# Hash-bucketed attention with two mixing layers: reciprocals spread a period later, bits placed a period earlier, x loaded through GpSimd's queue, three transpose banks

## The chip, the cores and the metric

The kernel runs on one core of a Trainium2 chip. The metric is the device time of one execution in microseconds (us), the median of several runs. The engines are TensorE (PE in the profile, PEld for its weight loads), VectorE (DVE), ScalarE (ACT), GpSimd (POOL) and SyncE (SP), which here only issues DMAs. GpSimd issues DMAs too, from the same in-order instruction stream in which it computes.

## What is computed

Everything is float32. Attention has batch 2, 8 heads, 768 positions and head size 64; a key counts for a query only if both fall in the same of 64 hash buckets:

```python
q_bits = (einsum('bhsd,dk->bhsk', q, proj) > 0)      # 6 bits
k_bits = (einsum('bhsd,dk->bhsk', k, proj) > 0)
mask = q_bucket[:, :, :, None] == k_bucket[:, :, None, :]
scores = where(mask, scale * q @ k.T, -1e9)
attn = exp(scores - max); attn = attn / (sum(attn) + 1e-9)
x = attn @ v                                          # -> (2, 768, 512)
xk, xr = mix of x with x shifted by one position
x = sigmoid(xr @ w_r) * (relu(xk @ w_k) ** 2 @ w_v)
h = relu(x @ w_in); u, v = halves of h
out = (u * (w_spatial @ layernorm(v) + b_spatial)) @ w_out
```

## The kernel before

Two stages follow each other: `attention` and `mixers`. Attention treats the 16 heads as 8 pairs. A pair has 12 units: two halves of the 768 queries, two heads e, and three blocks of 128 queries each, so 96 units in all; six units (one pair, one half) form a group g. Work goes in 32 periods of three units: the loop `for p in range(np3)` (L516) writes out by hand the order of every engine's instructions, each engine works its own stream in order, and a pair takes periods 4n to 4n+3.

For one unit, `scores` (L314) multiplies in TensorE into a bank pair of `ps_s`; the operands in `TK` hold the head's values in two parts, and the bits of the buckets in spare rows, so that one product gives score and mask. `peak` and `bias` (L330, L339) take the maximum on VectorE while copying the scores out of PSUM; `expo` (L345) is the exponential on ScalarE with the row sums in `den`; `transp` (L357) transposes three blocks of 128x128 into one bank of `ps_t`, and `evac` (L365) copies that bank out on ScalarE. A unit has two such moves. `ps_t` has two banks. `av` (L391) multiplies with v into one of two output banks, `obank[g % 2]`, twelve matmuls a period (`av3`), and lags by three periods. `recip` (L375) takes the reciprocals of a group's row sums on VectorE, transposes them, writes them to DRAM in four small DMAs (tile `ds`) and reads them back in two, spread over partitions (tile `rb`); `finish` (L401) multiplies them into the output bank on VectorE.

For a pair to come, `load_x` (L236, one DMA on SP, one buffer) and `load_pair` (L241, four DMAs on GpSimd) fetch it; `split_piece` (L254, eight on GpSimd) makes the low parts. `bits_mm` (L271) projects x in TensorE into `obank[0]`, `bits_sign` (L279, VectorE) makes bits of it (tile `zb`), `bits_scale` (L285, GpSimd) scales them (`zc`), and `bits_place` (L290) copies them into `TK` with eight DMAs on SP. SP's stream holds, in this order of planning: ds and rb, weight loads, placed bits, x and v; a DMA whose wait isn't over holds up those behind it.

Between these steps stands other work, put into half periods by `at_slot(p, k, job)` (L416): 12 weight blocks of the mixers (`weight_jobs`, L30: load, ScalarE and VectorE steps, the last two on GpSimd), two more in the last periods, and the first block of the mixers' inputs (`mix_jobs`, L130: `before`, a multiplication, on GpSimd; `full` on VectorE; `parts` on ScalarE and GpSimd). `bank` (L162) gives the mixers their output banks in turn from `ps_s`, `ps_t` and `obank`.

## Time and profile before

| | us |
|---|---|
| runs shown | 593.57, 601.83, 590.88 |
| median | 593.57 |
| profiled execution, its own time | 593.77 |
| its span on the core | 592.0 |

The span is what the trace covers, from its first to its last instruction; times of rows are counted from its start. A row of the timeline has start, length, engine, line, operation, output and inputs, a count of merged instructions, and in brackets the idle time before it with what ended it. A wait is put down to what came last.

### The profile page before, as it was taken

The numbers are of one execution on the slowest core, as the hardware profiler recorded it, in microseconds if no ns is written. First come the engines' busy times: TensorE is split into PE (matmuls) and PEld (weight loads), VectorE is DVE, ScalarE is ACT, GpSimd is POOL, SyncE is SP. The second block draws the span as 40 slices with busy tenths as digits, with TensorE's granted clock in tenths as the row PEclk, the third lists the DMA queues.
The fourth block names the chain that finished last, engine by engine and source line by source line (L and its number), as shares of the span: only waits on it lengthen the run. The fifth ranks groups of instructions, "written<-read, shape, count | busy, mean of one in ns | idle before, by whom it ended". The sixth has DMA issues, their size and how long they took to land.

```text
span 592.0 us, 8973 instructions
## 1 busy us (share of the span) xinstructions
PE 555.9 (94%) x3188; PEld 471.3 (80%) x3188; DVE 375.7 (63%) x804; ACT 337.8 (57%) x718; POOL 147.9 (25%) x154
## 2 busy tenths in 40 slices
PE   6879997998999899889979999999999999999997
PEld 5766665666666566658979999999999899999996
DVE  6547985776757687953986557342799687272240
ACT  1867887677777778854965275643743552221112
POOL 5554576265636473540000000000020000000000
PEclk8889999899999999989989999999999999999999
DMA  8984295619293923102222021100175210001102
GB/s 166 223 169 127 63 234 97 171 48 219 74 195 98 197 62 99 40 1 85 73 71 72 2 71 37 37 1 1 37 227 179 66 53 2 0 2 54 53 19 89
DMA packets 21245, 51.96 MB, mean 88 GB/s; under 512 B 3840, under 2 KB 6864, under 8 KB 21200
## 3 DMA queue, kind: packets, MB, share of 16 engines
q1 hardware_dynamic: 15584, 36.42, 20.7%
q0 software_dynamic: 5472, 14.94, 13.1%
q8 instruction: 25, 0.41, 0.3%
q14 instruction: 20, 0.16, 0.1%
q10 hardware_dynamic: 144, 0.02, 0.0%
HBM read 47.08 MB, written 3.19 MB: 85 GB/s over the span
## 4 chain that ended last, share of the span: by engine, by line
PE 67%; DVE 9%; DMA 9%; ACT 7%; issue 4%; POOL 3%; SPq 1%; POOLq 0%; DVEq 0%; ACTq 0%
PE o L176 16%; PE v L626 8%; PE s L324 7%; PE t L362 6%; PE s L176 6%; PE o L393 5%; PE k L176 5%; DMA tk<-zc 5%; PE w L176 4%; PE u L176 4%; PE r L176 3%; DVE p L334 3%; PE o L626 3%; DMA w_raw<-in_w_k_dram 2%; ACT PT L368 2%
## 5 line engine op out<-in xcount | busy, mean ns | idle before, releaser
L334 DVE TENSOR_SCALAR_CACHE_REDUCE p<-s 128x768 f32<-128x768 f32 x96 | 91.5, 953 | 58.4 <-PE s L324 53.9
L368 ACT COPY PT<-t 128x384 f32<-128x384 f32 x192 | 84.8, 475 | 45.4 <-PE t L362 45.3
L362 PE MATMUL t<-ident,p 128*128 128x128 f32 x576 | 85.2, 285 | 17.2 <-ACT PT L368 16.4
L324 PE MATMUL s<-tk 128*128 128x384 f32 x384 | 89.6, 367 | 10.3 <-DMA tk<-zc 7.3
L352 ACT ACTIVATE p<-p,nb 128x768 f32<-128x768 f32 x96 | 90.2, 940 | 12.9 <-DVE nb L342 12.1
L324 PEld LDWEIGHTS s<-tk 128*128 128x128 f32 x384 | 66.9, 197 | 34.9 <-issue 9.7
L362 PEld LDWEIGHTS t<-ident,p 128*128 128x128 f32 x576 | 67.0, 144 | 32.0 <-ACT PT L368 25.8
L393 PE MATMUL o<-PT,v 128*64 128x384 f32 x384 | 69.6, 499 | 0.0
L258 POOL TENSOR_TENSOR tk<-x,tk 64x384 fp32r<-64x384 f32 x56 | 58.5, 1070 | 31.7 <-DMA x<-in_kq_dram 23.6
L626 PE MATMUL v<-k,wv 128*128 128x384 f32 x288 | 53.9, 335 | 0.6 <-DVE k L592 0.6
L626 PEld LDWEIGHTS v<-k,wv 128*128 128x128 f32 x288 | 50.3, 188 | 0.9 <-DVE k L592 0.9
L393 PEld LDWEIGHTS o<-PT,v 128*64 128x64 f32 x384 | 25.0, 138 | 29.2 <-issue 29.1
L685 POOL DMA_DIRECT2D wsp<-in_w_spT_dram x6 | 3.6, 606 | 174.8 <-DVE w_a L44 168.3
L176 PE MATMUL k<-tk,wk 128*128 128x384 f32 x252 | 45.5, 334 | 0.0
L176 PE MATMUL o<-wk,tk 128*128 128x512 f32 (+1 forms) x204 | 44.8, 377 | 0.0
L176 PEld LDWEIGHTS k<-tk,wk 128*128 128x128 f32 x252 | 43.9, 188 | 0.0
L176 PEld LDWEIGHTS o<-wk,tk 128*128 128x128 f32 x204 | 36.8, 188 | 6.9
L592 DVE TENSOR_TENSOR k<-kt,k 128x384 fp32r<-128x384 f32 x32 | 17.8, 556 | 22.1 <-ACT k L610 22.0
L176 PE MATMUL r<-tk,wr 128*128 128x384 f32 x144 | 27.7, 342 | 3.0 <-DVE tk L122 1.9
L150 DVE SCALAR_TENSOR_TENSOR f<-XT,msc,d 128x384 f32<-128x384 f32 x32 | 21.2, 661 | 13.7 <-ACT d L144 9.0
L121 ACT CAST tk<-g 128x384 fp32r<-128x384 f32 x16 | 8.2, 515 | 37.5 <-DVE g L756 37.5
L176 PEld LDWEIGHTS r<-tk,wr 128*128 128x128 f32 x144 | 25.1, 189 | 5.3 <-DVE tk L122 2.4
(107 smaller groups left out, 892.4 us busy)
## 6 DMA issues: line engine op xcount, KB each, us to landing
tk<-in_kq_dram POOLq DMA_DIRECT2D x32, 384.0 KB, 7.3
x<-in_kq_dram SPq DMA_DIRECT2D x8, 768.0 KB
w_raw<-in_w_k_dram SPq DMA_DIRECT2D x8, 512.0 KB
w_raw<-in_w_v_dram SPq DMA_DIRECT2D x8, 512.0 KB
w_raw<-in_w_in_dram SPq DMA_DIRECT2D x8, 512.0 KB
v<-in_vP_dram SPq DMA_DIRECT2D x8, 384.0 KB
rb<-ds SPq DMA_DIRECT2D x32, 96.0 KB
out_dram<-ot SPq DMA_DIRECT2D x11, 256.0 KB
```

What stands on the lines that cost most here:

```text
L121: nc.scalar.copy(hi, src)
L150: nc.vector.scalar_tensor_tensor(st["f"], x, mu, st["d"], op0=ALU.mult, op1=ALU.add)
L176: nc.tensor.matmul(o, a, x, start=(i == 0), stop=(i == len(seq) - 1))
L258: nc.gpsimd.tensor_sub(tk[l, 1 + 2 * t, o], raw[pp][l, t, o], tk[l, 2 * t, o])
L324: nc.tensor.matmul(s[:, c, :HS], w, t[:, n, c * HS:(c + 1) * HS], start=(n == 0), stop=(n == 1),)
L334: nc.vector.tensor_scalar(c, s[:, :, :HS], -BIG / 2, None, op0=ALU.max, op1=ALU.max, accum_out=m)
L352: nc.scalar.activation(c, c, AF.Exp, bias=nb, scale=0.125, accum_out=den[g][:, u:u + 1])
L362: nc.tensor.transpose(t[:, 128 * n:128 * n + 128], p[:, k0:k0 + 128], ident)
L368: nc.scalar.copy(PT[g][:, e, 3 * c:3 * c + 3, 128 * j:128 * j + 128], t[:, :HS].rearrange("p (n q) -> p n q", n=3),)
L393: nc.tensor.matmul(obank[g % 2][64 * e:64 * e + 64, :HS], vt[g // 2][:, kt, e, :], PT[g][:, e, kt, :], start=(kt == 0), stop=(kt == 5),)
L592: later(lag, lambda: eng.tensor_sub(lo, src, hi))
L626: nc.tensor.matmul(os[m][:, :HS], w, x, start=(c == 0 and k == 0), stop=(c == 7 and k == 2),)
```

## The change

Six things change. `ps_t` gets a third bank and `obank` is one bank instead of two; the bits' product goes to a `ps_t` bank, and the mixers' rotation `bank` is adapted. `load_x` goes through GpSimd's queue for pairs 2 to 7. `recip` ends with the write of ds; the read of rb becomes `spread`, one period later, on SP, and `recip` stands ahead of the jobs of its half period. `finish` moves from the first half of period 2g+5 to the second half of 2g+4. The bits' steps move forward: product, sign and scale to the first half of the pair's second period (they were in the second half of the second and the first half of the third), the placing to the second half of the second period (was the third). The first mix block's `before` goes from GpSimd to VectorE, with lags of 0, 0 and 1 half periods instead of 0, 1 and 2.

```diff
-    ps_t = ctx.enter_context(tc.tile_pool(name="ps_t", bufs=2, space=PS))
+    ps_t = ctx.enter_context(tc.tile_pool(name="ps_t", bufs=3, space=PS))
-    obank = [ps_o.tile([128, 512], F32, name=f"o{n}") for n in range(2)]
+    obank = ps_o.tile([128, 512], F32, name="o0")
...
-        n = turn[0] % (2 if turn[0] < 8 else 3)
+        n = turn[0] % (2 if turn[0] < 8 else 6)
...
-        if n == 0:
+        if n % 3 == 0:
             return ps_s.tile([128, 2, 512], F32, tag="s", name=name)[:, 0, :]
-        if n == 1:
+        if n != 2:
             return ps_t.tile([128, 512], F32, tag="t", name=name)
-        return obank[turn[0] // 3 % 2]
+        return obank
...
-            nc.sync.dma_start(raw[pp], kq[b, p].rearrange("t r s -> r t s"))
+            (nc.gpsimd if pp > 1 else nc.sync).dma_start(raw[pp], kq[b, p].rearrange("t r s -> r t s"))
...
         def bits_mm(pp):
+            zs[pp] = ps_t.tile([128, 512], F32, tag="t", name="z")
             for g in range(4):
...
-                    obank[0][32 * g:32 * g + 32, :HS], pb, raw[pp][:, 1 - g // 2, o:o + HS],
+                    zs[pp][32 * g:32 * g + 32, :HS], pb, raw[pp][:, 1 - g // 2, o:o + HS],
...
                 nc.sync.dma_start(ds[:, 32 * n:32 * n + 32], rt[32 * n:32 * n + 6, :])
+            R[g] = ds
+
+        def spread(g):
+            ds = R[g]
             R[g] = at.tile([128, 3, 128], F32, tag="rb", bufs=2, name="rb")
...
-                    obank[g % 2][64 * e:64 * e + 64, :HS],
+                    obank[64 * e:64 * e + 64, :HS],
...
-            jobs = mix_jobs(mid, 0, which, 4 * which, 2, nc.gpsimd)
-            for job, lag in zip(jobs[3 * c:3 * c + 3], (0, 1, 2)):
+            jobs = mix_jobs(mid, 0, which, 4 * which, 2, nc.vector)
+            for job, lag in zip(jobs[3 * c:3 * c + 3], (0, 0, 1)):
...
-                at_slot(p0 + 1, 1, lambda n=pp + 1: bits_mm(n))
-                at_slot(p0 + 2, 0, lambda n=pp + 1: bits_sign(n))
-                at_slot(p0 + 2, 0, lambda n=pp + 1: bits_scale(n, nc.gpsimd))
-                at_slot(p0 + 2, 1, lambda n=pp + 1: bits_place(n))
+                at_slot(p0 + 1, 0, lambda n=pp + 1: bits_mm(n))
+                at_slot(p0 + 1, 0, lambda n=pp + 1: bits_sign(n))
+                at_slot(p0 + 1, 0, lambda n=pp + 1: bits_scale(n, nc.gpsimd))
+                at_slot(p0 + 1, 1, lambda n=pp + 1: bits_place(n))
...
             if p >= 3:
                 av3(p - 3)
-            if p >= 5 and p % 2:
-                finish((p - 5) // 2)
+            if p >= 2 and p % 2 == 0:
+                recip(p // 2 - 1)
             for job in plan.pop((p, 0), ()):
                 job()
-            if p >= 2 and p % 2 == 0:
-                recip(p // 2 - 1)
+            if p >= 3 and p % 2:
+                spread((p - 3) // 2)
...
             score(a + 2)
             expo(a + 2)
+            if p >= 4 and p % 2 == 0:
+                finish((p - 4) // 2)
...
         r_group(0, 1, mid)
+        spread(np3 // 2 - 1)
         av3(np3 - 2)
```

The warm-up matmuls and the sign follow the renamed banks and are left out here.

## Rows read from the trace of the kernel before

**Rows 1.** The page's first part: busy time, share of the span and instructions of each engine.
```profile
PE 555.9 (94%) x3188; PEld 471.3 (80%) x3188; DVE 375.7 (63%) x804; ACT 337.8 (57%) x718; POOL 147.9 (25%) x154
```
**Rows 2.** Busy time by stretch (start:end, length, then busy us and instructions of each engine, TensorE's granted clock as a share of full speed, mean busy share of the DMA engines, GB/s).
```profile
50.00:250.00 200.00, 183.09 (x1152) 126.91 (x1152) 150.48 (x363) 152.60 (x341) 108.26 (x105) 0.99 0.51 121
...
265.00:592.00 327.00, 319.97 (x1747) 304.49 (x1745) 187.62 (x357) 146.11 (x295) 3.60 (x6) 0.99 0.17 56
```
**Rows 3.** Waits between 40 and 250 us: who waited for whom, us in total, times, the longest.
```profile
PE t L362 <- ACT PT L368: 11.3, 29, 2.4
```
**Rows 4.** The timeline of TensorE's matmuls: the bits' product at the end of period 21, the first rows of periods 22 and 23, the second half of period 23, and the first row of period 24.
```profile
179.25 0.85 PE L274 MATMUL o<-x,msc 128*32 128x384 f32 x8
180.03 1.68 PE L324 MATMUL s<-tk 128*128 128x384 f32 x8
...
186.98 1.64 PE L324 MATMUL s<-tk 128*128 128x384 f32 x8
...
191.29 0.98 PE L324 MATMUL s<-tk 128*128 128x384 f32 x4
192.10 0.82 PE L362 MATMUL t<-ident,p 128*128 128x128 f32 x6
193.16 0.93 PE L362 MATMUL t<-ident,p 128*128 128x128 f32 x6 [0.24 <-ACT PT L368]
193.85 1.64 PE L324 MATMUL s<-tk 128*128 128x384 f32 x8
```
**Rows 5.** The same timeline where periods 4, 12, 21 and 25 begin and where the next ones do (period 22 begins in the second line of rows 4).
```profile
40.27 0.60 PE L324 MATMUL s<-tk 128*128 128x384 f32 x2
...
48.91 1.65 PE L324 MATMUL s<-tk 128*128 128x384 f32 x8
...
100.37 0.60 PE L324 MATMUL s<-tk 128*128 128x384 f32 x2
103.95 2.29 PE L324 MATMUL s<-tk 128*128 128x384 f32 x6 [2.98 <-DMA tk<-zc]
...
111.85 1.64 PE L324 MATMUL s<-tk 128*128 128x384 f32 x8
...
171.10 0.77 PE L324 MATMUL s<-tk 128*128 128x384 f32 x3
...
200.75 0.59 PE L324 MATMUL s<-tk 128*128 128x384 f32 x2
...
211.14 1.66 PE L324 MATMUL s<-tk 128*128 128x384 f32 x8
```
**Rows 6.** Busy time by stretch as in rows 2, of two slices of 5 us.
```profile
65.00:70.00 5.00, 4.76 (x31) 2.97 (x31) 4.90 (x10) 3.59 (x9) 4.84 (x5) 1.00 0.49 159
...
105.00:110.00 5.00, 5.00 (x26) 3.42 (x26) 3.48 (x11) 2.70 (x6) 0.00 (x0) 0.81 1.07 312
```
**Rows 7.** The timeline of SP's queue: DMAs issued, with the time that issuing took.
```profile
166.09 0.46 SPq L239 DMA_DIRECT2D x<-in_kq_dram  x1
...
189.60 6.23 SPq L305 DMA_DIRECT2D tk<-zc  x8
...
198.82 1.30 SPq L383 DMA_DIRECT2D ds<-rt  x4
207.48 1.13 SPq L386 DMA_DIRECT2D rb<-ds  x2
```
**Rows 8.** The timeline around period 17: SP's issue of a weight block for it, and TensorE.
```profile
135.93 0.39 SPq L37 DMA_DIRECT2D w_raw<-in_w_k_dram  x1
...
140.35 1.66 PE L324 MATMUL s<-tk 128*128 128x384 f32 x8
...
148.67 0.93 PE L362 MATMUL t<-ident,p 128*128 128x128 f32 x6 [2.36 <-ACT PT L368]
...
150.31 1.66 PE L324 MATMUL s<-tk 128*128 128x384 f32 x8
```
**Rows 9.** Single lines of the kernel: least, median and greatest length in ns of GpSimd's tk issues (each 384 KB, half of an x load), the time from issue to landing of all 32 tk loads (the line of the view for that tile), and three VectorE operations: one with one input, f of the mix, and finish.
```profile
L246 POOL DMA_DIRECT2D tk<-in_kq_dram x16: 583/632/742, 1.2 to 194.4; - x16
...
DMA to landing us min/median/max: 4.3/7.3/12.8
...
L62 DVE TENSOR_SCALAR w_p<-w_b x32: 412/419/1126, 45.2 to 455.6; 128x512 uint32<-128x512 uint32 x32
...
L150 DVE SCALAR_TENSOR_TENSOR f<-XT,msc,d x32: 600/618/1354, 231.8 to 391.8; 128x384 f32<-128x384 f32 x32
...
L406 DVE TENSOR_TENSOR XT<-o,rb x16: 533/558/561, 52.2 to 270.2; 128x384 f32<-128x384 f32 x16
```
**Rows 10.** The timeline of GpSimd: the first piece that waits for x (period 21), the scaling of bits in period 22, and the first tk issue in period 23.
```profile
175.99 4.77 POOL L258 TENSOR_TENSOR tk<-x,tk 64x384 fp32r<-64x384 f32 x4 [9.87 <-DMA x<-in_kq_dram]
...
185.15 1.24 POOL L287 TENSOR_SCALAR zc<-zb,msc 128x384 fp32r<-128x384 f32 x1 [4.39 <-issue]
...
193.17 0.66 POOL L246 DMA_DIRECT2D tk<-in_kq_dram  x1
```
**Rows 11.** The timeline of VectorE and TensorE in period 31, the last of attention.
```profile
254.61 0.94 DVE L334 TENSOR_SCALAR_CACHE_REDUCE p<-s 128x768 f32<-128x768 f32 x1
...
251.97 0.96 PE L324 MATMUL s<-tk 128*128 128x384 f32 x4
...
257.29 1.54 PE L362 MATMUL t<-ident,p 128*128 128x128 f32 x6 [2.52 <-ACT PT L368]
```
## What the change should do to the time

> **What bounds the kernel now.** I read the page's busy shares first [rows 1], then the busy times by stretch [rows 2], then TensorE's waits inside attention, and last TensorE's rows in order of time. The first says TensorE, the second more: after 265 us it is busy 319.97 of 327 us, and the change alters only which bank the groups rotate through there, so that stage keeps its time. Between 50 and 250 us TensorE is busy 183.09 of 200 us, while ScalarE has 152.60 and VectorE 150.48. So nearly all that can be won is TensorE's idle time in attention (17 us in those 200) and the slow clock after long idle stretches.
>
> The timeline [rows 4] shows one period p of three units (p = 23, from the 8 score products at 186.98 to those at 193.85: 6.87 us, my base). The reader is to see the one break of TensorE's work in it: 6 transposes end, then 0.24 us until ScalarE has emptied a transpose bank. Bits add 0.78 us once in four periods (179.25 to 180.03). Summed from 40 to 250 us that wait is 11.3 us in 29 times [rows 3], once in each period and two more. The other wait, for placed bits, is in the next part [rows 5].
>
> **What is removed: the bits' wait.** Length of the four periods with such a wait, less 6.87 and less 0.78 for bits where they are computed [rows 4, 5]: p4 48.91 - 40.27 = 8.64, over by 1.77; p12 111.85 - 100.37 = 11.48, over by 4.61 (2.98 idle, and then the next 6 score products take 2.29 us where 6 of 8 take about 1.2: the granted clock is 0.81 of 2.4 GHz from 105 to 110 [rows 6], so part ran at 1.2 GHz); p21 180.03 - 171.10 = 8.93, over by 1.28; p25 211.14 - 200.75 = 10.39, over by 2.74. Sum 10.4 us.
> Why they wait: GpSimd scales the bits at 185.15 (1.24 us) [rows 10], SP begins to place them only at 189.60, and needs 6.23 us for 8 placements [rows 7]; the first half is wanted from 193.85 on, the second from 200.75, when p25 begins. p25 runs over by 2.7, so the last, issued at 195.1, is down only about 203.4, 8.3 us later. In the changed order z is computed behind av, at +4.3 us in its period (where scores(a+2) stood, 191.29 - 186.98 [rows 4]), plus 0.8, 0.6 for the sign (as f, of as many columns [rows 9]) and 1.24 for the scale: placing begins about 7 us into period 4n-3 and ends at 13.3; even with 8.3 us to land the first half is down at 18.4 and the second at 21.6, while they are wanted at 20.6 and 27.5. The tk and x loads, beside which it took so long, now come later than the placements, so it should land sooner. Taken: all 10.4 us; bounds 5.9 (p4 and p25 stay) and 10.4.
>
> **The transposes' third bank.** Two banks make the third transpose group wait for the first one's copy. With three it starts at once; the fourth then asks for the first bank 0.41 us later (6 transposes, 0.82 us for two groups [rows 4]), when its copy, late by 0.24, is done. TensorE gains 0.24 per period. Some of the 29 are longer and have other causes (the longest, 2.4, is costed below), so I count 26 plain periods of the 29 from 3 to 31: 26 x 0.24 = 6.2; I take 6.0. Bounds: nothing, if ScalarE or VectorE set the period instead, and 7.5. z now takes a turn in the same banks; its reader, the sign, is through 0.6 us after bits, under scores and one transpose group (0.98 + 0.4): no cost. The one output bank left: finish(g) now stands in the second half of period 2g+4 and av of the next group in the first half of 2g+5, some 4 us of scores and transposes later [rows 4]: no cost while rb is there.
>
> **SP without x and without the wait for ds.** Spread no longer holds SP until ds lands (198.82 to 207.48 is the case [rows 7]), and x leaves SP's queue. In p17 ScalarE's copies, and through them TensorE for 2.36 us, wait behind a step on a weight block that SP issued at 135.93, right behind x [rows 8]: that period is 150.31 - 140.35 - 0.78 - 6.87 = 2.31 over. Planned for the second half of period 15 and issued 2.4 us into period 16, the load can now go out in its place. Taken 1.7, bounds 0 and 2.3.
> x through GpSimd: six issues. No x issue on GpSimd is shown; the nearest, half the size, take 0.58 to 0.74 us [rows 9], so 0.6 to 1.5 each on an engine busy 108.26 of 200 us [rows 2]. Queued behind each are the tk loads and the next pair's pieces. GpSimd gets there about where it issued tk (193.17, 6.2 us into p23 [rows 10]; x now goes first). TensorE asks for x two periods later at +4.3, so 2 x 6.87 + 4.3 - 6.2 = 11.8 us after issue. The longest x load took 175.99 - 166.09 = 9.9 us [rows 7, 10]. So 1.9 us to spare, cost 0.
> The Trainium skill speaks against this step: "SBUF — State Buffer", section "SBUF: two separate sides", has VectorE's two-port operations lock GpSimd out of writing descriptors, about 620 ns alone against 3100 under a copy, and advises ACT's or SP's queue. By that figure, as an estimate, 2.5 us would come on top of each issue, 0.6 more than is to spare, 3.6 us over six pairs. The trace doesn't show it so far: the longest of 16 issues on that line is 0.74 us [rows 9], with VectorE busy 75% of the stretch.
>
> **The end of attention.** Eight multiplications of the mix go from GpSimd to VectorE; none is there to see with one SBUF input of 384 columns, the nearest (512 columns) has a median of 0.42 and a maximum of 1.13 [rows 9], so 0.35 each alone, 1.1 at worst. In p31 the last maximum starts at 254.61, 1.7 us after the scores' end (251.97 + 0.96), and TensorE idles 2.52 and then runs 6 transposes in 1.54 instead of 0.93 us [rows 11]. Ahead of that maximum finish (0.56) leaves, f, which takes 1.35 at most, may come down to its median of 0.62 without GpSimd's multiplication beside it [rows 9], and one multiplication of 0.35 joins: 0.56 + 0.73 - 0.35 = 0.9 gained. Waits of f on GpSimd go too, put at 0.4. Taken 1.3; bounds -2 (all eight at 1.1 in the way) and 4.
> **The beginning.** z of pair 1 is asked for some 4 us earlier; x of pair 1 may not have landed. But sign and reciprocals no longer stand before a maximum in p2. Taken 0.3; bounds -2 and 1.5.
>
> **What comes back.** VectorE is busy 4.90 of 5 us in single slices [rows 6], where its operations run beside GpSimd's; there 0.25 us less per period turns into a wait for VectorE. I take 1.0 us; its bound is all 6 of the bank's gain.
>
> **Sum**, against the profiled execution's own 593.8 us (592.0 of span and 1.8 around it; the median shown is 593.57, 0.2 less): 10.4 + 6.0 + 1.7 + 1.3 + 0.3 - 1.0 = 18.7; 593.8 - 18.7 = 575.1, said as 575.
>
> **Rivals.**
> A. *The bits' waits go, but VectorE and ScalarE set the period*, so that the bank brings nothing: 593.8 - (10.4 + 1.7 + 1.3 + 0.3) = 580.1. For it: the slices at 4.90. Against it: over 200 us both stand at 75%, some 1.7 us idle in each period of 6.87. Chance 0.20.
> B. *The bits still land late*, because SP now holds spread at its head while ds waits behind weights and v (8.7 us of wait have been seen [rows 7]): 593.8 - 8.3 = 585.5. Against it: placing starts 7 us earlier, and x is off this queue. Chance 0.08.
> C. *Slower: TensorE waits for x.* Place: bits of pairs 2 to 7, which stand in TensorE's order ahead of scores(a+2). With x landing L us after issue each costs L - 11.8, six times. The gain is eaten at L = 11.8 + 18.7/6 = 14.9, and 2% slower begins at 16.9; L = 18 would give 575.1 + 37.2 = 612. For it: tk, half the bytes, has taken up to 12.8 us [rows 9]; double that is 25.6. The skill's rule above adds to L. Against it: x now stands ahead of tk in GpSimd's queue, and beside both of them it took 9.9 us. Chance 0.08, five eighths of it beyond 16.9.
> The forecast has the remaining 0.64, its own range 568 to 581 from the bounds above.
>
> **How the numbers follow.** Predicted 575. Low end: the upper bounds, 10.4 + 7.5 + 2.3 + 4 + 1.5 with nothing coming back, make 25.7, or 568; 2 us more for waits not listed: 566. High end: A and B are inside, B with one of the smaller terms failing besides: 588. C remains outside. A measurement here tells apart about 2%, 12 us: 581.7 is the border. Faster by over 2%: the forecast's 0.62 and two thirds of A, 0.13: 0.75. Slower by over 2%: 0.05 from C. Within: 0.20.
>
> **What would show it.** Right: no wait of the scores for placed bits; periods without bits near 6.6 us; the wait for the transposes' copy nearly gone; the granted clock without the dip near 105 us; bits with no wait for x; spread issued without a pause. Wrong: TensorE or VectorE waiting for x or rb, placements landing after period 4n begins, periods still at 6.87 with the idle time elsewhere, or a GpSimd whose pieces end after the scores ask for them.

## The result, and the profile after

The changed kernel takes 574.65 us (median of 4 runs, 572.43 to 575.92), the kernel before beside it 594.88 us (590.88 to 601.83): ratio 0.968, 95% interval 0.961 to 0.974, faster. Run once more on another chip it gave 573.09 us, ratio 0.957 (0.954 to 0.959). The forecast was 575 in a range of 566 to 588. The profiled execution took 572.43 us, its span 570.7, against 592.0: 21.3 us less, where the sum said 18.7.

The page's busy shares of the changed kernel answer to [rows 1]:
```profile
PE 548.7 (96%) x3188; PEld 468.0 (82%) x3188; DVE 378.0 (66%) x812; ACT 336.4 (59%) x718; POOL 143.2 (25%) x152
```
Its busy time by stretch (columns as in [rows 2]): attention's middle, all after attention, and its last two slices of 5 us.
```profile
50.00:230.00 180.00, 174.62 (x1124) 122.78 (x1123) 151.98 (x363) 150.06 (x339) 105.65 (x105) 1.00 0.56 131
240.00:570.70 330.70, 324.02 (x1763) 308.51 (x1762) 187.70 (x358) 146.86 (x296) 3.61 (x6) 0.99 0.16 53
230.00:235.00 5.00, 1.88 (x11) 1.44 (x9) 4.08 (x11) 2.98 (x9) 1.13 (x1) 0.79 0.00 0
235.00:240.00 5.00, 5.00 (x16) 1.88 (x16) 0.49 (x1) 2.53 (x4) 1.99 (x2) 0.52 0.50 152
```
TensorE is now busy 97% of the middle (before 92%), and that at full clock. The last two slices are attention's end: TensorE is mostly idle, then works from 235 to 240 at a granted clock of 0.52, that is near the lower of its two levels (1.2 of 2.4 GHz).

TensorE's waits from 40 to 235 us, to set beside [rows 3]:
```profile
PE t L364 <- ACT p L354: 4.9, 8, 2.9
PE s L326 <- DVE p L336: 1.8, 3, 0.8
PE t L364 <- ACT PT L370: 1.7, 4, 0.8
```
The wait for the transposes' copy, 9.2 us before in these 195 us, is 1.7. No wait for placed bits is left, and none for x. In their place stand short waits for the exponential and, behind it, for VectorE's maximum. One plain period of the changed kernel, to set beside [rows 4]:
```profile
186.50 1.64 PE L326 MATMUL s<-tk 128*128 128x384 f32 x8
187.97 0.82 PE L364 MATMUL t<-ident,p 128*128 128x128 f32 x6
188.72 2.16 PE L399 MATMUL o<-PT,v 128*64 128x384 f32 x12
190.81 0.97 PE L326 MATMUL s<-tk 128*128 128x384 f32 x4
191.62 1.61 PE L364 MATMUL t<-ident,p 128*128 128x128 f32 x12
192.98 1.66 PE L326 MATMUL s<-tk 128*128 128x384 f32 x8
```
The reader is to see the fifth line: the 12 transposes of the second half run as one block, where [rows 4] has two blocks with a break of 0.24 us. The period is 192.98 - 186.50 = 6.48 us, against 6.87.

**A measure for all versions.** A period's first `av` product is easy to find in TensorE's timeline. I call the time from that of period k to the next one stretch k; it lies about two thirds of a period ahead of the prediction's period k+1 (stretch 11 before is 11.48 us, as its p12). Each profiled execution splits into the time to the first `av` (start), the stretches 3 to 27 (middle), the stretches 28 to 32 (end, up to the last two `av3` after the loop), and the rest:

| us | start | middle | end | rest | span |
|---|---|---|---|---|---|
| before | 35.63 | 191.69 | 38.72 | 325.96 | 592.0 |
| changed | 30.81 | 171.38 | 41.74 | 326.77 | 570.7 |
| gain | 4.82 | 20.31 | -3.02 | -0.81 | 21.3 |

The middle's gain is 25 x 0.39 = 9.75 from the shorter plain period; 11.2 from the five stretches that had waited for bits (3, 7, 11, 20, 24: 8.60, 8.00, 11.48, 7.97, 9.48 before, 6.48 to 6.51 now); 2.1 from stretch 17 with its late weight block (9.96 against 7.85 for the other stretches with bits); about 1.2 from bits, which add 0.78 to a stretch now and added 0.98; 0.8 from small excesses before; less 4.7 of new ones: 171.38 - (25 x 6.48 + 6 x 0.78) = 4.70.

Those 4.70 lie in stretches 6, 10, 14, 15, 18, 19, 22 and 26; the largest, 22, is 8.02 us. The timeline of all engines of the changed kernel there (rows of TensorE, VectorE and GpSimd):
```profile
164.72 0.94 PE L326 MATMUL s<-tk 128*128 128x384 f32 x4
166.30 0.96 PE L326 MATMUL s<-tk 128*128 128x384 f32 x4 [0.63 <-DVE p L336]
167.61 0.91 PE L364 MATMUL t<-ident,p 128*128 128x128 f32 x6 [0.35 <-ACT p L354]
...
162.97 2.40 DVE L65 SCALAR_TENSOR_TENSOR w_a<-w_raw,w_p 128x512 f32<-128x512 uint32 x1
165.29 0.94 DVE L336 TENSOR_SCALAR_CACHE_REDUCE p<-s 128x768 f32<-128x768 f32 x1
...
158.29 6.47 POOL L258 TENSOR_TENSOR tk<-x,tk 64x384 fp32r<-64x384 f32 x6
```
A step of the weight split with two inputs from SBUF takes 2.40 us, where its median is 0.69, and ends 0.6 us after GpSimd's six pieces (158.29 + 6.47 = 164.76). The maximum behind it starts late, and TensorE waits for it and for the exponential.

### The profile page after: what moved, and what is told of

Same layout as the page of the kernel before. It is cut to its first block, busy times and chain, and to the rows that moved or that the text cites. A ratio compares the mean times of both kernels' runs of the same rounds, so it can differ in the third digit from the quotient of the medians.

```text
span 570.7 us, 8997 instructions
## 1 busy us (share of the span) xinstructions
PE 548.7 (96%) x3188; PEld 468.0 (82%) x3188; DVE 378.0 (66%) x812; ACT 336.4 (59%) x718; POOL 143.2 (25%) x152
## 4 chain that ended last, share of the span: by engine, by line
PE 76%; DVE 14%; ACT 5%; issue 3%; DMA 2%; SPq 0%; POOL 0%; DVEq 0%; ACTq 0%; POOLq 0%
PE o L176 11%; PE o L399 9%; PE t L364 8%; PE v L634 8%; PE s L326 8%; PE k L176 7%; PE s L176 7%; PE w L176 5%; PE u L176 5%; PE r L176 4%; DVE p L336 4%; PE o L634 3%; DVE w_a L65 2%; ACT p L354 2%; DVE f L150 2%
## 5 line engine op out<-in xcount | busy, mean ns | idle before, releaser
L326 PE MATMUL s<-tk 128*128 128x384 f32 x384 | 84.8, 354 | 4.3 <-DVE p L336 2.2
L364 PE MATMUL t<-ident,p 128*128 128x128 f32 x576 | 80.4, 279 | 8.4 <-ACT p L354 5.7
L176 PE MATMUL k<-tk,wk 128*128 128x384 f32 x336 | 59.6, 334 | 0.0
L176 PEld LDWEIGHTS k<-tk,wk 128*128 128x128 f32 x336 | 58.4, 188 | 0.0
L176 PE MATMUL r<-tk,wr 128*128 128x384 f32 x168 | 34.3, 361 | 2.3 <-DVE tk L122 1.7
L176 PEld LDWEIGHTS r<-tk,wr 128*128 128x128 f32 x168 | 31.8, 204 | 5.5 <-DVE tk L122 2.3
L176 PE MATMUL o<-wk,tk 128*128 128x512 f32 (+1 forms) x168 | 36.2, 374 | 0.0
L176 PEld LDWEIGHTS o<-wk,tk 128*128 128x128 f32 x168 | 30.0, 188 | 5.5
L615 ACT ACTIVATE kr<-k 128x384 f32<-128x384 f32 x28 | 13.6, 487 | 33.0 <-PE k L176 32.8
L176 PE MATMUL w<-wk,tk 128*128 128x512 f32 x132 | 30.7, 390 | 0.0
```

The costliest lines, as they stand in the source:

```text
L176: nc.tensor.matmul(o, a, x, start=(i == 0), stop=(i == len(seq) - 1))
L326: nc.tensor.matmul(s[:, c, :HS], w, t[:, n, c * HS:(c + 1) * HS], start=(n == 0), stop=(n == 1),)
L364: nc.tensor.transpose(t[:, 128 * n:128 * n + 128], p[:, k0:k0 + 128], ident)
L615: nc.scalar.activation(r, o[:, :HS], AF.Relu)
```

## The experiments

Twelve kernels ran, each compared with the kernel before on the same chip; the changed kernel once more stands among them. "Middle" is to be compared with 171.4, "end" with 41.7, and the kernel before with 191.7 and 38.7. The three parts come from one profiled execution each, and the kernel before was profiled on the first chip alone; the ratios come from several runs on one chip. Start and end differ by up to 2.6 us with the clock that the one execution was granted there.

| version | us | ratio, 95% interval | start | middle | end |
|---|---|---|---|---|---|
| changed, again | 573.09 | 0.957 (0.954 to 0.959) | 32.49 | 171.37 | 41.45 |
| two transpose banks | 590.92 | 0.986 (0.978 to 0.994) | 33.94 | 183.94 | 41.37 |
| bits in their old slots | 583.25 | 0.974 (0.967 to 0.981) | 33.67 | 178.36 | 40.61 |
| x on SP | 578.02 | 0.966 (0.960 to 0.972) | 35.19 | 180.99 | 40.66 |
| spread at once | 578.33 | 0.964 (0.961 to 0.967) | 33.78 | 175.65 | 40.63 |
| mix on GpSimd, old lags | 569.52 | 0.951 (0.946 to 0.956) | 34.11 | 171.41 | 35.62 |
| mix on VectorE, old lags | 571.28 | 0.954 (0.951 to 0.956) | 33.20 | 171.37 | 38.99 |
| mix on GpSimd, late weights earlier | 568.32 | 0.949 (0.946 to 0.951) | 32.63 | 171.40 | 35.71 |
| before + bits' slots alone | 585.66 | 0.982 (0.975 to 0.989) | 33.77 | 185.48 | 36.97 |
| before + third bank alone | 594.47 | 0.993 (0.989 to 0.997) | 34.65 | 193.58 | 39.38 |
| mix on GpSimd, no pieces | 566.32 | 0.947 (0.941 to 0.952) | 32.80 | 167.15 | 37.13 |
| mix on GpSimd, pieces earlier | 583.97 | 0.972 (0.965 to 0.980) | 35.43 | 186.56 | 35.55 |

### The transposes' banks

The changed kernel with the two output banks and two transpose banks of before:
```diff
-    ps_t = ctx.enter_context(tc.tile_pool(name="ps_t", bufs=3, space=PS))
+    ps_t = ctx.enter_context(tc.tile_pool(name="ps_t", bufs=2, space=PS))
```


> The changed kernel with two transpose banks again (the output bank that is thereby free goes back into the mixers' rotation, which is that of before). Base: 574.6. Theory now, from the trace after: a plain period is 6.48 us against 6.87, so the third bank is worth 0.39 in each of 29 periods, 11.3 us, of which some 4 were lost again to waits on VectorE, which vanish here: 582 to 586, plain period 6.87, waits on VectorE in periods 7, 11, 15, 23 and 27 gone. The prediction's size of this term (0.24 in 26 periods): 580.6, the other 0.15 per period coming from SP and the bits: plain period near 6.72. Rival, the bank buys nothing: 574 to 575.

The plain period is back at 6.87 and the middle 12.6 us longer. Its waits of TensorE, in the same stretch of time as above:
```profile
PE t L365 <- ACT PT L371: 9.8, 31, 0.7
PE s L327 <- DVE p L337: 2.3, 2, 1.2
```
25 x 0.39 = 9.75 of the 12.6 is the break in each period; the rest is what stretches 6, 14, 18 and 22 run over by (9.31, 8.15, 7.81, 9.34), less what 10, 15 and 26 no longer do. So the theory's size of the bank holds, but the waits on VectorE did not vanish as it said: there are fewer, and longer ones.

The other way round, the kernel before with a third bank (one output bank, bits in the transposes' pool, `finish` in the second half of period 2g+4) and nothing else:


> The kernel before with one part of the change alone: a third transpose bank, with one output bank, bits in the transposes' pool, and finish moved to the second half of the even period as that needs. Bits' slots, x through SP, the spread at once, the mix on GpSimd all stay. Theory (the bank is worth 0.39 us per plain period, since the fourth transpose group's wait of 0.11 goes as well as the third's): plain periods fall from 6.87 to 6.48, mid-attention from 191.7 by 7 to 10 us to 182 to 185, with the waits for tk<-zc still there; ratio 0.982 to 0.989. Rival of the prediction (0.24 per period): plain periods at 6.63 and mid-attention 185 to 187. Rival (the time goes into the wait for placed bits, as these land at a time that SP sets): mid-attention stays above 188, with the waits for tk<-zc longer than before.

Plain stretches do fall to 6.48 (8, 14, 16, 18), and yet the middle is 1.9 us longer than before: the signs of the last rival are there. TensorE's waits from 40 to 235 us in this version:
```profile
PE s L326 <- DMA tk<-zc: 12.9, 9, 3.7
PE t L364 <- ACT PT L370: 0.9, 1, 0.9
```
The wait for the copy is gone and the wait for placed bits has grown from 7.3 us (5 times) to 12.9 (9 times), with slow clock after it: stretch 11 takes 13.00 us, 24 takes 11.48. When the bits land is set elsewhere, and a TensorE that gets there sooner only waits longer. The 1.9 us are one execution against one on another chip; by ratio the version is 0.7% (0.3 to 1.1%) faster, some 4 us. So the bank alone brings far less than its 9.75 us, and whether it brings nothing or 4 us in the middle is not shown.

### The bits' slots

The changed kernel with the bits in their old slots:
```diff
-                at_slot(p0 + 1, 0, lambda n=pp + 1: bits_mm(n))
-                at_slot(p0 + 1, 0, lambda n=pp + 1: bits_sign(n))
-                at_slot(p0 + 1, 0, lambda n=pp + 1: bits_scale(n, nc.gpsimd))
-                at_slot(p0 + 1, 1, lambda n=pp + 1: bits_place(n))
+                at_slot(p0 + 1, 1, lambda n=pp + 1: bits_mm(n))
+                at_slot(p0 + 2, 0, lambda n=pp + 1: bits_sign(n))
+                at_slot(p0 + 2, 0, lambda n=pp + 1: bits_scale(n, nc.gpsimd))
+                at_slot(p0 + 2, 1, lambda n=pp + 1: bits_place(n))
```


> The changed kernel with the bits' four steps in their old half periods; x through GpSimd, spread a period later and three banks stay. Base: 574.6. Theory of the prediction, the waits for placed bits go because placing starts a period earlier: they return in some pairs, since placing would end some 6 us into the pair's fourth period and take 2 to 8 us to land: 577 to 583, scores waiting for placed bits 2 to 8 us in total. Rival, SP's relief from x and from the wait for ds was enough: 574 to 575.5, and no such wait.

The middle is 7.0 us longer, mostly in stretches 4, 12 and 13 (9.66, 9.86, 9.01). But the wait has another name than before: TensorE waits for tk<-zc only 1.9 us, and VectorE 11.5 us in three times for rb. SP's queue, and VectorE's row that waits, in this version:
```profile
94.80 2.24 SPq L307 DMA_DIRECT2D tk<-zc  x3
97.08 1.16 SPq L392 DMA_DIRECT2D rb<-ds  x2
...
107.59 0.56 DVE L411 TENSOR_TENSOR XT<-o,rb 128x384 f32<-128x384 f32 x1 [5.00 <-DMA rb<-ds]
```
Spread goes out behind the placings, and is down only 107.59 - 97.08 = 10.5 us later: x and tk of the next pair were issued from 94.42 to 97.6, and the DMA share is 1.48 from 100 to 105. Then `finish` stands at VectorE's head, and the maxima behind it wait. TensorE waits too, 3.3 us in two times, because `av` needs the one output bank that `finish` has not emptied: the second output bank, given up for the third transpose bank, costs nothing only as long as rb is there.

The kernel before with the bits' new slots alone:


> The kernel before with one part of the change alone: bits, their sign, scale and placings go to the earlier slots of the changed kernel. Two transpose banks, x through SP's queue, the spread at once, the mix's multiplications on GpSimd all stay. Theory (the wait for placed bits was 10.4 us, and comes off by the earlier slots): TensorE no longer waits for tk<-zc, periods 4, 12, 21 and 25 lose 1.8, 4.6, 1.3 and 2.7 us over their base of 6.87 + 0.78, and the kernel is 6 to 10 us faster, ratio 0.983 to 0.990; mid-attention (periods 3 to 27) falls from 191.7 to 182 to 186 us. Rival (the placings, two periods earlier, now stand ahead of the loads on SP and the wait only changes its name): TensorE waits for x or VectorE for rb, as in the run with the late placings, and mid-attention stays above 187 us, ratio above 0.992.

The theory holds: no wait for tk<-zc, middle 185.48, 6.2 us less. That isn't all 11.2: the excess is now in stretches 6, 14, 18 and 22 (9.59, 8.40, 8.07, 9.59), the ones that ran over with two banks above. Stretch 17, whose late weight block the prediction put down to SP without x, is plain here too (7.64, before 9.96), although x and the spread are as before: behind the earlier placings SP issues that block at 125.61 instead of 135.93. VectorE and GpSimd in stretch 22 of this version, and TensorE's row that waits:
```profile
176.30 1.39 DVE L65 SCALAR_TENSOR_TENSOR w_a<-w_raw,w_p 128x512 f32<-128x512 uint32 x1
177.61 2.21 DVE L377 TENSOR_SCALAR rc<-den 128x6 f32<-128x6 f32 x1
...
171.62 6.93 POOL L258 TENSOR_TENSOR tk<-x,tk 64x384 fp32r<-64x384 f32 x6
...
181.20 0.96 PE L324 MATMUL s<-tk 128*128 128x384 f32 x4 [1.42 <-DVE p L334]
```
An operation on six columns takes 2.21 us there; the median of its line is 0.17. GpSimd's pieces, and its operation behind them, run beside VectorE's steps here; that they meet because the bits are scaled earlier is likely, but no run parts it.

### The queues: x on GpSimd, spread a period later

The changed kernel with every x load on SP again:
```diff
-            (nc.gpsimd if pp > 1 else nc.sync).dma_start(raw[pp], kq[b, p].rearrange("t r s -> r t s"))
+            nc.sync.dma_start(raw[pp], kq[b, p].rearrange("t r s -> r t s"))
```


> The changed kernel with all x loads on SP. Base: 574.6. Theory: SP isn't held up any more, x goes out between spread and v in the pair's fourth period and lands before it is asked for 18 us later, so 573.5 to 576, with TensorE not waiting for x. Rival, x through GpSimd is what keeps ds and rb prompt: ds lands behind x in the same queue, spread holds SP 8 to 10 us and the placed bits or rb come late: 578 to 585, with waits of scores for placed bits or of VectorE for rb.

The profiled execution took 584.78 us, the slowest of its six, so its sums are too high to be used. Its waits: VectorE for rb 9.5 us in three times, the longest 6.1, and stretches 4, 5 and 12 of 10.92, 9.70 and 7.63; TensorE for the output bank 5.4 us in two times, and for x once, 1.8. By ratios it lies 1.0% above the changed kernel of the other chip and within the interval of the first comparison, so how much x on GpSimd brings is not settled; no comparison shows that it costs anything. GpSimd's issues of x in the changed kernel, and the times from issue to landing (least, median, greatest):
```profile
L239 POOL DMA_DIRECT2D x<-in_kq_dram x6: 787/791/800, 32.2 to 170.1; - x6
...
DMA to landing us min/median/max: 5.0/6.6/8.9
```
At most 0.80 us to issue and 8.9 to land, against the 11.8 that the prediction had from the issue to TensorE's need. The Trainium skill's figure for a lock ("SBUF — State Buffer", section "SBUF: two separate sides": 3100 ns beside a VectorE copy, 620 alone) is not seen in any of the six, with VectorE busy 84% of the middle; whether one of VectorE's operations beside them was of the kind that the page means, no run shows.

The changed kernel with ds read back at once, as before:
```diff
-            R[g] = ds
-
-        def spread(g):
-            ds = R[g]
```


> The changed kernel with rb read back right behind the writes of ds again, so that SP stands until ds has landed; all else stays. Theory of the prediction (a step to free SP, worth little once x is off the queue and the bits are a period early): 0 to 3 us slower than the changed kernel, no or short waits of scores for placed bits. Rival, the later spread is what keeps the placed bits in time: 4 to 10 us slower, scores waiting for placed bits over 3 us in total.

Beside the changed kernel on the same chip (0.957) this is 0.8% or 5.2 us more: the rival's size, but not its cause, for no score waits for placed bits. The middle is 4.3 us longer, and 4.0 of it in one place, stretch 4 (10.50 against 6.52). SP's queue in this version, and the rows of ScalarE and TensorE that wait:
```profile
34.11 1.16 SPq L388 DMA_DIRECT2D rb<-ds  x2
35.31 0.59 SPq L37 DMA_DIRECT2D w_raw<-in_w_r_dram  x1
...
45.83 0.66 ACT L41 ACTIVATE w_a<-w_raw 128x512 f32<-128x512 f32 x1 [2.58 <-DMA w_raw<-in_w_r_dram]
...
46.91 0.55 PE L364 MATMUL t<-ident,p 128*128 128x128 f32 x3 [2.60 <-ACT PT L370]
```
The weight block stands behind rb, goes out at 35.31, in the midst of x and tk (33.77 to 38.3), and is down after 10.5 us. In the changed kernel it goes out at 30.29, ahead of them. In the other pairs the stretches are those of the changed kernel.

### The end of attention

The changed kernel with the mix as before the change:
```diff
-            jobs = mix_jobs(mid, 0, which, 4 * which, 2, nc.vector)
-            for job, lag in zip(jobs[3 * c:3 * c + 3], (0, 0, 1)):
+            jobs = mix_jobs(mid, 0, which, 4 * which, 2, nc.gpsimd)
+            for job, lag in zip(jobs[3 * c:3 * c + 3], (0, 1, 2)):
```


> The changed kernel with the eight multiplications of the first mix block on GpSimd again, and their old lags of 0, 1 and 2 half periods. Base: 574.6. Theory from the trace after, VectorE is overfull in the last three periods: 8 x 0.41 us leave it and the last period shrinks from 12.0 towards 10.3: 571 to 573.5. The prediction's view, the move to VectorE gains 1.3 us: 575.5 to 576.5.

The end takes 35.62 us instead of 41.74; the middle stays at 171.4. The last rows of attention in the changed kernel (TensorE, then what VectorE does ahead of the last maximum), to set beside [rows 11]:
```profile
227.90 0.96 PE L326 MATMUL s<-tk 128*128 128x384 f32 x4
...
233.88 1.54 PE L364 MATMUL t<-ident,p 128*128 128x128 f32 x6 [2.89 <-ACT p L354]
235.35 4.11 PE L399 MATMUL o<-PT,v 128*64 128x384 f32 x12
...
229.34 0.69 DVE L65 SCALAR_TENSOR_TENSOR w_a<-w_raw,w_p 128x512 f32<-128x512 uint32 x1
229.95 0.41 DVE L146 TENSOR_SCALAR d<-XT,omu 128x384 f32<-128x384 f32 x1
230.47 1.17 DVE L150 SCALAR_TENSOR_TENSOR f<-XT,msc,d 128x384 f32<-128x384 f32 x1
231.56 0.94 DVE L336 TENSOR_SCALAR_CACHE_REDUCE p<-s 128x768 f32<-128x768 f32 x1
```
and TensorE in the version with the mix on GpSimd:
```profile
229.30 0.97 PE L326 MATMUL s<-tk 128*128 128x384 f32 x4
...
233.85 0.91 PE L364 MATMUL t<-ident,p 128*128 128x128 f32 x6 [1.82 <-ACT p L354]
234.69 2.16 PE L399 MATMUL o<-PT,v 128*64 128x384 f32 x12
```
In the changed kernel the last scores are ready at 228.9 and their maximum starts at 231.56, 2.7 us later (1.7 before): behind three steps of the weight split, d and f of the mix stand in the way (before, `finish` and f), and f takes 1.17 us. TensorE idles 2.89 us instead of 1.82, and after it the clock is low: the next 6 transposes and 12 products of `av` take 1.54 + 4.11 instead of 0.91 + 2.16, 2.6 us more. These 2.6 us are not the price of the longer idle time alone. At the same place the version without pieces (below) idles 1.82 us as well and then has the low clock:
```profile
228.17 1.52 PE L364 MATMUL t<-ident,p 128*128 128x128 f32 x6 [1.82 <-ACT p L354]
229.62 3.14 PE L399 MATMUL o<-PT,v 128*64 128x384 f32 x12
```
So of the 6.1 us between the two ends 2.6 hang on the clock of one execution each, and 3.5 are the change's. By ratios (0.957 and 0.951) the two kernels are 0.6% apart, 3.6 us.

To part the engine from the lags: the mix on VectorE with the old lags.


> The changed kernel with the mix's multiplications on VectorE but the old lags of 0, 1 and 2 half periods, so that engine and lag are told apart. Theory, it is VectorE's load that costs: the stretch from period 28's av to period 32's end stays near 41.7 us (35.6 with the multiplications on GpSimd). Rival, it is the shorter lags: that stretch falls to 36 to 38 us.

The end takes 38.99, between the two, and the ratio, 0.954, lies halfway between 0.957 and 0.951 as well: the shorter lags and VectorE's eight multiplications cost about 0.3% each, 1.8 us, though the intervals of neighbours overlap. Of the 2.7 us that the lags cost in the profiles, 1.2 lie in stretch 28 (7.72 us, here 6.48), where f stands ahead of a maximum and takes 1.51 us; about 1 is clock, for here too TensorE idles 2.90 us before the last transposes, which with `av` then take 1.47 + 3.20. At the last maximum the lags change nothing: d and f stand ahead of it in both.

And one attempt at more, on the version with the mix on GpSimd: the two late weight blocks a period earlier (`p0 = np3 - 4 + n` for `np3 - 3 + n`).


> The changed kernel with the mix's multiplications on GpSimd with the old lags, and with the two early weight blocks of the last three periods begun one period sooner (28 and 29 instead of 29 and 30). Theory, VectorE is overfull in periods 29 to 31 (three steps of 1.8 us of a weight block stand before the last maximum): the stretch from period 28's av to period 32's end, 35.6 us in the run with the mix on GpSimd alone, falls by 1 to 2.5 us, and the time to about 1.0 to 2.5 us under that run's, ratio to before 0.947 or so. Rival, period 28 has no room either: no change against that run.

The end is 35.71; what leaves one stretch (31: 6.31 for 7.47) comes back in another (30: 9.19 for 8.20). Of all versions that compute everything this and the mix on GpSimd with its weights as they were are the fastest, and not to be told apart: 0.949 and 0.951.

### What came back in the middle

The version with the mix on GpSimd, without GpSimd's pieces for pairs 2 to 7 (it leaves out the low parts of their operands):
```diff
-                for k in range(8):
+                for k in range(8 if pp == 0 else 0):
```


> The version with the mix's multiplications back on GpSimd, and with GpSimd's 48 subtractions for the low parts of pairs 2 to 7 left out, so that part of the scores' low terms is missing. Theory (what came back in the middle, 4.4 us over 25 plain periods of 6.48 us, comes from VectorE's operations with two SBUF inputs running beside GpSimd's pieces): the excess of periods 7, 11, 15, 23 and 27 goes, mid-attention falls from 171.4 to 166.5 to 168.5 us, and the weight split's scalar_tensor_tensor on VectorE is never much over its 0.7 us alone. Rival (VectorE's own load sets those periods, whatever GpSimd does): the excess stays, mid-attention at 170.5 us or more. A kernel about 3 to 5 us faster than the version with the pieces (569.5) by the theory, within 1 us of it by the rival.

The theory is right. The middle falls to 167.15, 0.5 us above 25 x 6.48 + 6 x 0.78 = 166.68; every one of its stretches is within 0.16 us of 6.48 or 7.26. (The end is 1.5 us longer, 37.13: it is the low clock after the last idle time, 1.52 + 3.14 us instead of 0.91 + 2.16, shown above. The whole is 3.2 us below the version with the pieces.) The weight split's step on VectorE between 40 and 240 us (least, median, greatest in ns), with the pieces:
```profile
L65 DVE SCALAR_TENSOR_TENSOR w_a<-w_raw,w_p x14: 648/694/2404, 42.6 to 230.4; 128x512 f32<-128x512 uint32 x14
```
and without them:
```profile
L65 DVE SCALAR_TENSOR_TENSOR w_a<-w_raw,w_p x14: 647/692/1032, 41.3 to 224.7; 128x512 f32<-128x512 uint32 x14
```
So the excess needs GpSimd beside VectorE; VectorE's own load doesn't make it. This agrees with the Trainium skill ("SBUF — State Buffer", section "Who interferes with whom"), by which a VectorE instruction with two inputs from SBUF contends with a GpSimd instruction that reads SBUF, and the one that comes second waits: 0.69 us alone, 2.40 beside the pieces. The step waited longer than for one piece (1.0 us): it began within one and ended 0.6 us after the next.

With the pieces kept, but a period earlier (four of them ahead of the scaling of bits):


> The version with the mix's multiplications on GpSimd, and with GpSimd's eight subtractions for the next pair a period earlier: four of them ahead of the scaling of bits, where GpSimd now stands idle for up to 10 us, and four behind it. Everything is computed. Theory (the 4.7 us that came back come from the subtractions beside VectorE's two-input steps of the weight split): which stretches run over changes with the place of the subtractions; those that now run over (6, 10, 14, 15, 22 and 26) get to within 0.2 us of 6.48 or of 7.26, others may run over in their place, and mid-attention comes to 168 to 171 us against 171.4, the kernel to 567 to 570. Rival (the stretches run over for another reason, such as ScalarE's or VectorE's own steps in them): the same stretches run over by the same amounts, mid-attention at 171 or more. Rival (the subtractions ahead of the scaling wait for the tk loads, which have taken up to 13.9 us to land, and hold the scaling of bits up): the placings get late, TensorE waits for tk<-zc, and mid-attention is above 173.

None of the three is quite right. Of the six stretches named, 6 and 15 come to 6.54 and 6.59; 10, 14, 22 and 26 run over by more than they did (7.41, 7.67, 8.87, 7.24), with the weight split's step at 2.63 us in stretch 22, again beside the pieces and GpSimd's operation behind them. So the excess moves with the pieces, but can't be moved out of the way by a period: the weight split is there too. And a new loss is larger than all of it, stretch 4 of 17.50 us. GpSimd, SP's queue and VectorE there:
```profile
29.22 3.90 POOL L258 TENSOR_TENSOR tk<-x,tk 64x384 fp32r<-64x384 f32 x4 [8.29 <-DMA tk<-in_kq_dram]
33.22 1.25 POOL L289 TENSOR_SCALAR zc<-zb,msc 128x384 fp32r<-128x384 f32 x1
...
34.49 6.07 SPq L307 DMA_DIRECT2D tk<-zc  x8
40.67 1.42 SPq L385 DMA_DIRECT2D ds<-rt  x4
...
49.42 1.16 SPq L392 DMA_DIRECT2D rb<-ds  x2
...
55.40 0.56 DVE L411 TENSOR_TENSOR XT<-o,rb 128x384 f32<-128x384 f32 x1 [9.22 <-DMA rb<-ds]
```
GpSimd issued x and tk from 38.83 to 42.0. ds, written from 40.67 on, is waited for until 49.42; rb comes down 6.0 us after it. In the changed kernel the scaling stands at 21.39, ds of the same group goes out at 28.84, ahead of the loads (32.2 to 35.4), rb at 31.25, and `finish` doesn't wait. So the last rival is half right: the pieces wait 8.29 us for tk and hold the scaling up, and with it the placings and, behind them on SP, ds. Its wait has another name: TensorE never waits for tk<-zc, VectorE waits for rb.

The second run of the changed kernel was to part luck from gain at the start:


> The changed kernel itself, beside the kernel before and the next three runs on one chip, so that differences of 1% can be read. Theory: ratio to before 0.961 to 0.974 as measured. In the profile the first av (period 3) stands at 33 to 35.5 us and not at 30.8 as in the first profile of it, because that start was an accident of TensorE's clock: it stood at 35.6 before and at 33.7 to 35.2 in three variants that don't touch the start. Rival, the start is faster by the change: 30.8 again.

Its start is 32.49 with a granted clock of 0.66 from 10 to 20 us, as before (35.63, 0.66); the first profile has 30.81 with 1.00. So of the 4.8 us some 1.7 go with the clock of that one execution; 32.49 is still 0.5 us below what the theory gave. Over all versions in the table the start is 32.5 to 35.4.

## Why the prediction was right, step by step

The time held, 575 forecast and 574.65 measured, and so did the cause: the waits of TensorE inside attention. Several terms were mis-sized, and the errors cancelled: that the time came within half a microsecond is luck.

- **Bits' wait, 10.4.** Right: 11.2 measured in the first comparison of profiles. It left stretch 7 (1.1 us) out. But it is not the slots' alone: undone alone they lose 7.0 in the middle, done alone they gain 6.2 (2.3 of it stretch 17, which the prediction counts under SP). Rival B named the place, SP's queue; with the old slots the wait came back there, as one for rb.
- **Third bank, 6.0.** The step that failed is "TensorE gains 0.24 per period". The 0.24 is read from the idle column, and that understates the break. Before the change, at the break of [rows 4]:
```profile
192.65 0.27 PE L362 MATMUL t<-ident,p 128*128 128x128 f32 x1
193.16 0.33 PE L362 MATMUL t<-ident,p 128*128 128x128 f32 x1 [0.24 <-ACT PT L368]
```
  Within a block a transpose starts 0.11 us after the one ahead of it, though each row is 0.27 long. Here 0.52 pass from start to start, 0.41 too many; the idle column counts only from the row's end. Over the whole second half, twelve transposes took 1.99 us before (192.10 to 193.16 + 0.93) and take 1.61 now, so 0.38 of the 0.39 per plain period is here. The theory of the third bank alone put what is over 0.24 down to a wait of the fourth group that goes; that isn't so. This group waits more now: it starts 0.19 us after the transpose ahead of it, before 0.11. The bank's 9.75 over the 25 stretches is above the upper bound of 7.5. It is worth that only with the bits' wait gone: alone it made the kernel 0.7% faster by ratio, with a middle 1.9 us longer in its profile, where bits' slots alone gain 6.2 and the whole change 20.3.
- **SP relief, 1.7.** The size is right, 2.1, but the cause is not shown to be this: with the bits' slots alone, x and spread as before, stretch 17 loses its excess too (7.64), and with the bits in their old slots and SP relieved it does as well (7.47). Either is enough. "Spread issued without a pause" was wrong: SP still waits for ds, 41.0 us in 19 times in the changed kernel. It has become harmless: `finish` waits for rb nowhere in the middle, and the placings no longer come late behind it. With spread at once the middle loses 4.3, nearly all in stretch 4, which no term had.
- **x through GpSimd, 0.** Right in size: 0.79 us an issue, 8.9 us at most to land. Rival C did not occur.
- **End of attention, +1.3 (bounds -2 to 4).** Wrong, below its bound: the end is 3.0 us longer, though it has the bank's gain in it; against the old mix 6.1. The multiplication was sized well (0.41, 0.35 forecast). What failed is "f may come down to its median of 0.62": f took 1.17 us with no multiplication of the mix on GpSimd, and 1.51 in stretch 28; GpSimd's other operations ran beside it both times (L122 at 230.09 for 1.13 us, L77 at 205.10 for 1.31). The term also left out what the shorter lags do in stretch 28, 1.2 us. And the working stopped at idle time: up to 2.6 us of low clock came on top, a price that differs from execution to execution.
- **Beginning, 0.3.** 4.8 in the first profile, 3.1 in the second at the same granted clock as before; the runs scatter by 3 us, so its true size is open between about 0 and 3.
- **What comes back, -1.0 (bound 6).** 4.7, for the reason given, VectorE beside GpSimd; the bound held, the size didn't. Rival A's mechanism was thus there, at a small scale: not the engines' load but that they stand in each other's way.

Against the profiled executions: bank +3.8, bits +0.8, bits' own product +1.2, SP +0.4, small excesses +0.8, beginning +4.5, against end -4.3, what comes back -3.7 and the rest -0.8: 2.7 more than the sum's 18.7, the 21.3 of the spans but for rounding.

## What to carry to other kernels

The idle column is not the whole of a break: it counts from the end of a row, where the next operation would have started before that end. Compare starts, or the length of a whole block with its like (1.99 against 1.61 us for twelve transposes), before a buffer's worth is counted. Gains of a bank and of earlier data don't add: a faster engine runs into the next late transfer (middle +1.9 and -6.2 us alone, by single profiles; together with the queues' relief -20.3), so take away the late transfer first. Work that is moved to an engine with idle share is not free where that engine stands last in the chain: eight multiplications of 0.41 us and a lag shorter by half a period cost some 3.5 us at attention's end, and the mix left on GpSimd makes the whole change 0.95 instead of 0.957 to 0.968. And before a difference of 2 us between two profiles is given to a change, look whether the same rows ran at the same clock in both.

## What the runs showed of the hardware

DMAs that SP issues while x and tk of a pair are on their way landed late: rb took 10.5 us in one version and 6.0 in another, a weight block 10.5 in a third, each with a DMA share near or above 1 in those slices. At attention's end, with no such loads, the last rb took 4.7 and 5.0 us in two versions whose `finish` waits for it (pieces earlier, mix on GpSimd). They landed late although the loads stood in GpSimd's queue and not in SP's. That the loads are the cause is read from the order of the rows in all three; no run took the loads alone away.

VectorE's operations with one input also grow beside GpSimd: rc<-den on six columns took 2.21 us, median 0.17, and the weight split's clamp (L44) has a median of 0.77 us in the middle with GpSimd's pieces and 0.42 without them. GpSimd's issues of x did not grow: 0.787 to 0.800 us.

The same idle time at attention's end was followed by either clock. After 1.82 us the 12 products of `av` took 2.16 us in two versions (mix on GpSimd, pieces earlier), 3.14 and 3.85 in two others (no pieces, third bank alone); after 2.52 us 2.99 in the kernel before, 2.16 with the bits' slots alone; after 2.88 to 2.90 us, in seven profiles, 3.09 to 4.11. The granted clock of those 5 us was 0.52 in the changed kernel (235 to 240), 0.68 with the old lags, and 1.00 with the mix on GpSimd. What decides between the two levels is open.
